# Second scores of four token groups in one exp, doubled by DMA; softmax sums and parts of h through the gate ring

## Chip, cores, metric

One NeuronCore of one Trainium2 chip. The metric is device microseconds (us) of one execution; lower is better. PE is TensorE, ACT ScalarE, DVE VectorE, POOL GpSimd and SP SyncE; PSUM is the memory that PE writes its results to.

## The reference, cut to what matters

```python
# x: (4, 12416, 128) fp32; inducing: (32, 128); moe weights 128x1536, 128x1536, 1536x128
def mab(q, kv):
    s = (q @ kv.transpose(0, 2, 1)) / sqrt(128)
    a = exp(s - s.max(-1)); a /= a.sum(-1)
    return a @ kv
h = mab(inducing, x)             # 32 rows per batch: first attention
y = mab(x, h)                    # 12416 tokens per batch: second attention
out = (relu(y @ w_gate) * (y @ w_val)) @ w_out      # hidden width 1536
```

## The kernel before

Four batches, here called blocks (b = 0 to 3). Tokens go in groups of 512. A **pair** is two groups, a **quad** is four. (Two or four blocks per exp mean groups.)

The hidden weights are multiplied once per block with h (`hgv`), so that the gate and value of a token need only its 32 second scores: `p2` (exp of x times h) against `hgv`. The scores' sum `z2` is not divided out until the end; the result is scaled with 1/z2 twice. A **unit** is 128 hidden columns for a pair: two gate matmuls and two value matmuls (K = 32), two relus on ACT (`g`), one product on DVE (`gv`). Each **slot** of the hand-made schedule issues one unit: 147 slots per block, 588 in all. Twelve products feed an output chain of twelve full 128x128x512 matmuls in one PSUM bank.

PSUM has three rings (a ring is a few buffers that are used in turn): "g" with three banks for gates, "v" with two double banks for values, "o" with one bank for the output chain. The gates ring also takes **guests**: things that PE writes and ACT copies or exponentiates, and that need a bank for a moment.

```python
def bank(tag, name, shape=None, dtype=FP32):
    return psum.tile(shape or [P, BLK], dtype, tag=tag,
                     bufs={"g": 3, "v": 2, "o": 1}[tag], name=name)

def s2_pe(hT, xT, pr):                       # second scores of one pair, hT holds h twice
    ps = bank("g", "s2_ps")
    for k in range(2):
        t0 = (2 * pr + k) * TPB
        nc.tensor.matmul(ps[64*k : 64*k+64, :], hT, xTs(xT, t0, TPB), start=True, stop=True)
    return ps
def s2_exp(ps, pr):
    p2 = st([P, BLK], FP16, "p2", 4)
    nc.scalar.activation(out=p2, in_=ps, func=AF.Exp, scale=sm_scale)
    return p2
def z2_pe(p2s):                              # sums of the second softmax, in the OUTPUT bank
    ps = bank("o", "z2_ps", [P, 2, TPB, 2], FP32)
    for j, p2 in enumerate(p2s):
        for t in range(TPB):
            nc.tensor.matmul(ps[:, j, t, :], p2[:, t*P:(t+1)*P], sel, start=True, stop=True)
    return ps
```

While block b runs, the first attention of block b+1 ("phase 1") is prepared in between, in six parts and a rest: x is loaded and cast (`x16`), transposed by DMA (`xT`), scored (`s1T`, a guest), exponentiated (`p1T`), transposed by DMA (`p1g`), and used for h:

```python
def act():                                   # first exp, with its row sums from the accumulator
    p1T = st([P, BLK], FP16, "p1T", 2)
    nc.scalar.activation(out=p1T, in_=ps, func=AF.Exp, scale=sm_scale,
                         accum_out=s["zp"][:, q:q+1])
    def tr():
        p1g = st([P, TPB, P], FP16, "p1g", NQ)
        nc.sync.dma_start_transpose(out=p1g, in_=p1T)
        s["p1g"][q] = p1g
    post[at + 2].append(tr)
...
def h_part(q):                               # all parts in ONE group of the output bank, late
    if q == 0: s["h_ps"] = bank("o", "h_ps", [P, P], FP32)
    for t in range(TPB):
        for r in range(4):
            nc.tensor.matmul(ps[32*r : 32*r+32, :], s["p1g"][q][:, t, 32*r : 32*r+32],
                             s["x16"][:, q*CT + r*TPB + t, :], start=..., stop=...)
...
s["jobs"] = [ ([(at, lambda q=q: h_part(q)) for q in range(NQ + 1)], sums, ([1, 2, 2, 2],) * 2),
              ([(at, join)], finish, ([1], [1])) ]
```

`join` adds the four row groups of h (`hz_ps`), DVE divides (`hT`), and `hgv` of the next block is made. Output chains, z2, h and the join are **jobs**: they share the one output bank and follow each other. A finished chain goes on: ACT copies it out (`oT`), SP (SyncE) issues its DMA transpose (`o`), GpSimd scales it (`osb`), SP issues the store. SP thus issues loads, transposes and stores, all in one order fixed by the schedule.

The softmax here doesn't subtract the row's maximum and nothing guards it: scores larger than these inputs give would overflow.

## Time and profile before

| | before |
|---|---|
| time, median of 4 runs (range) | 753.06 us (749.74 to 754.89) |
| DVE, ACT, PE busy | 93%, 92%, 88% |
| mean granted PE clock | 0.969 |
| guests in the gate ring | 81 |

The prediction below shows the busy shares, the groups and the pace.

### The profile page before, as it was taken

Reading aid. Unit: us, or ns where it says so; the run is one execution under the profiler, and the core shown is the slowest. Engines: PE = TensorE matmul, PEld = TensorE weight load, DVE = VectorE, ACT = ScalarE, POOL = GpSimd, SP = SyncE. Lnnn points to the kernel's source line nnn. Section 1 sums busy time; section 2 is a strip of 40 time slices with the busy share of each in tenths; the row PEclk is TensorE's granted clock in tenths of the full one; section 3 lists DMA queues with packets and bytes.
Section 4 is the critical chain, followed back from the end, with each engine's and each line's share of the span. In section 5 each row is a group of like instructions: output and inputs, shape, how many; then the busy total and the mean of one; then the engine's idle time right before and its main releaser. Section 6 shows DMA issues by size and latency. Waiting matters only on the chain. (4 is left out here: it accounts for less than half of the span.)

```text
span 751.8 us, 13935 instructions
## 1 busy us (share of the span) xinstructions
PE 660.0 (88%) x4719; PEld 196.3 (26%) x4719; DVE 696.6 (93%) x670; ACT 690.2 (92%) x1393; POOL 211.7 (28%) x418
## 2 busy tenths in 40 slices
PE   4788998998988899898888899899898988898897
PEld 4422222222232222222222222222222222222222
DVE  3499999999999999999989999999999999999986
ACT  3589999998999999999899999999899999999985
POOL 3403323321234233222123333331122222222221
PEclk9869999999999999999999999999999999999999
DMA  8615555621135655642125556652112112122212
GB/s 340 211 24 163 128 136 134 155 69 44 50 120 139 154 142 147 143 102 59 42 80 138 162 127 146 161 129 60 37 49 64 57 55 65 45 63 63 65 43 69
DMA packets 121511, 78.51 MB, mean 104 GB/s; under 512 B 101952, under 2 KB 105056, under 8 KB 119136
## 3 DMA queue, kind: packets, MB, share of 16 engines
q1 hardware_dynamic: 121440, 77.63, 38.2%
q8 instruction: 37, 0.61, 0.3%
q14 instruction: 34, 0.28, 0.1%
HBM read 27.80 MB, written 25.43 MB: 71 GB/s over the span
## 5 line engine op out<-in xcount | busy, mean ns | idle before, releaser
L775 DVE TENSOR_TENSOR gv<-g,v_ps 128x1024 f16<-128x1024 f16 x576 | 669.5, 1214 | 27.1 <-PE g_ps L711 17.2
L772 ACT ACTIVATE g<-g_ps 128x512 f16<-128x512 f32 x1164 | 613.3, 616 | 34.5 <-PE g_ps L711 24.1
L514 PE MATMUL o_ps<-gv,wo 128*128 128x512 f16 x1128 | 341.3, 391 | 45.2 <-ACT oT L520 37.8
L711 PE MATMUL g_ps<-p,hgv 32*128 32x512 f16 (+1 forms) x1200 | 299.8, 382 | 3.5 <-ACT g L772 1.5
L531 POOL TENSOR_SCALAR osb<-o,z2i 128x128 f32<-128x128 f16 x376 | 164.0, 452 | 488.0 <-DMA o<-oT 322.5
L711 PE MATMUL v_ps<-p,hgv 32*128 32x512 f16 (+1 forms) x1200 | 236.2, 387 | 3.9 <-DVE gv L775 2.7
L514 PEld LDWEIGHTS <-wo 128*128 128x128 f16 x1176 | 82.7, 98 | 210.6 <-issue 178.8
L711 PEld LDWEIGHTS <-hgv 32*128 32x128 f16 x2400 | 65.8, 91 | 265.0 <-issue 259.3
L520 ACT CAST oT<-o_ps 128x512 f16<-128x512 f32 (+1 forms) x98 | 57.0, 582 | 0.0
L380 POOL CAST x<-x 128x2048 f16<-128x2048 f32 x18 | 34.1, 1892 | 13.2 <-DMA x<-in_x_dram 13.2
L171 ACT ACTIVATE p<-s_ps 128x512 f16<-128x512 f32 x48 | 29.2, 608 | 2.1 <-PE s_ps L161 2.1
L161 PE MATMUL s_ps<-xT,hT 128*64 128x512 f16 x96 | 21.5, 435 | 3.6
L251 DVE COPY xT<-xT_ps 128x1024 f16<-128x1024 f16 x12 | 8.3, 692 | 14.6 <-PE xT_ps L250 14.0
L250 PE MATMUL xT_ps<-eye,x 128*128 128x128 f16 x97 | 9.7, 257 | 9.2 <-ACT x L245 4.7
L258 ACT ACTIVATE p<-s_ps 128x256 f16<-128x256 f32 (+1 forms) x13 | 4.8, 370 | 12.1 <-PE s_ps L256 12.1
L181 PE MATMUL z_ps<-sel,p 128*128 128x2 f16 x192 | 8.2, 163 | 7.5 <-ACT oT L520 6.8
L161 PEld LDWEIGHTS <-hT 128*64 128x64 f16 x96 | 9.2, 110 | 18.9 <-issue 16.4
L181 PEld LDWEIGHTS <-p 128*128 128x128 f16 x192 | 8.1, 96 | 14.0 <-issue 13.5
L410 ACT ACTIVATE p1T<-s1T_ps 128x512 f16<-128x512 f32 x18 | 11.1, 619 | 0.0
L775 DVE TENSOR_TENSOR gvr<-g,v_ps 128x512 f16<-128x512 f16 x12 | 8.2, 686 | 2.6 <-PE g_ps L711 2.2
L250 PEld LDWEIGHTS <-x 128*128 128x128 f16 x97 | 7.1, 115 | 10.4 <-ACT x L245 5.4
L247 POOL CAST x<-gv 128x1024 f16<-128x1024 f32 x6 | 6.2, 1042 | 12.1 <-DMA gv<-in_x_dram 12.1
(83 smaller groups left out, 134.8 us busy)
## 6 DMA issues: line engine op xcount, KB each, us to landing
out_dram<-osb SPq DMA_DIRECT2D x94, 256.0 KB, 2.1
x<-in_x_dram SPq DMA_DIRECT2D x18, 1024.0 KB, 5.3
gv<-in_x_dram SPq DMA_DIRECT2D x12, 512.0 KB, 8.5
o<-oT SPq DMA_TRANSPOSE x98, 2.4
x<-in_moe_w_out_dram SPq DMA_DIRECT2D x1, 768.0 KB, 10.8
x<-in_moe_w_gate_dram SPq DMA_DIRECT2D x1, 512.0 KB, 9.5
x<-in_moe_w_val_dram SPq DMA_DIRECT2D x1, 512.0 KB, 9.6
out_dram<-osb SPq DMA_DIRECT2D x4, 128.0 KB, 1.7
```

The costliest lines, as they stand in the source:

```text
L161: nc.tensor.matmul(ps[64 * k : 64 * k + 64, :], hT, xTs(xT, t0, TPB), start=True, stop=True)
L171: nc.scalar.activation(out=p2, in_=ps, func=AF.Exp, scale=sm_scale)
L181: nc.tensor.matmul(ps[:, j, t, :], p2[:, t * P : (t + 1) * P], sel, start=True, stop=True)
L250: nc.tensor.transpose(ps[:, t - t0, :], x16[:, t, :], eye16)
L380: nc.gpsimd.tensor_copy(out=s["x16"][:, t0:t1, :], in_=s["x32", q])
L410: nc.scalar.activation(out=p1T, in_=ps, func=AF.Exp, scale=sm_scale, accum_out=s["zp"][:, q : q + 1])
L514: nc.tensor.matmul(c["ps"][:, 0:w], wo[:, i, :], gv(i), start=(i == 0), stop=(i == NFF - 1))
L520: nc.scalar.copy(out=oT[:, 0:w], in_=c["ps"][:, 0:w])
L531: nc.gpsimd.tensor_scalar(out=osb[:, t, :], in0=o16[:, t, :], scalar1=zz, scalar2=zz, op0=ALU.mult, op1=ALU.mult,)
L711: nc.tensor.matmul(ps[:, cols], hgv[:, s * P : (s + 1) * P], p2, start=True, stop=True)
L772: nc.scalar.activation(out=g16[:, k * BLK : (k + 1) * BLK], in_=ps, func=AF.Relu)
L775: nc.vector.tensor_tensor(out=ready["dst"], in0=ready["g16"][:, 0:n], in1=ready["v"][:, 0:n], op=ALU.mult)
```

## The change

Its intent, in four parts:

1. Second scores of a quad (four groups of 512) in one matmul pass and **one exp** (`p2q`) in place of two; each unit needs every score row twice, so eight small DMA copies on SP's queue double them.
2. The sums `z2` go through the gate ring (ACT copies them out, DVE inverts), not through the output bank.
3. h is made in seven separate guests of the gate ring; ACT copies each part out and GpSimd adds it up. PE makes the weight sums with a column of ones, so the accumulator reads fall away (21 of them before, 4.6 us of ACT; none after).
4. Output chains run at an even pace (1,2,2,2,2,3 matmuls per slot), with guests at the chain's second slot.

The diff, cut to its core:

```diff
+    def s2_quad_pe(hT, xT, qd):
+        ps = bank("g", "s2_ps")
+        for r in range(4):
+            nc.tensor.matmul(ps[32 * r : 32 * r + 32, :], hT[:, 0:M],
+                             xTs(xT, (4 * qd + r) * TPB, TPB), start=True, stop=True)
+        return ps
+    def p2_copies(p2q):
+        p2 = [st([P, BLK], FP16, "p2", 4) for _ in range(2)]
+        for j in range(2):
+            for k in range(2):
+                for d in range(2):
+                    nc.sync.dma_start(
+                        out=p2[j][64 * k + 32 * d : 64 * k + 32 * d + 32, :],
+                        in_=p2q[64 * j + 32 * k : 64 * j + 32 * k + 32, :])
+        return p2
 ... (cut)
+                ps = bank("g", "z2_ps", [P, TPB, 4])          # z2: was bank "o"
+                z2 = st(ps.shape, FP32, "z2" + tag, 2)
+                nc.scalar.copy(out=z2, in_=ps)
+                nc.vector.reciprocal(out=z2i, in_=z2)
 ... (cut)
-                    nc.scalar.activation(out=p1T, in_=ps, func=AF.Exp, scale=sm_scale,
-                                         accum_out=s["zp"][:, q : q + 1])
+                    nc.scalar.activation(out=p1T, in_=ps, func=AF.Exp, scale=sm_scale)
 ... (cut)
+        def h_part(at, q):
+            ps = bank("g", "h_ps", [P, P + 1])                # was one group in bank "o"
+            (4 matmuls with ones16[:, 0:1] into column P, 16 into columns 0 to P-1)
+            def act():
+                hq = st([P, P + 1], FP32, "hq", 2)
+                nc.scalar.copy(out=hq[0:n, :], in_=ps[0:n, :])
+                nc.gpsimd.tensor_tensor(out=s["hp"][0:n, :], in0=s["hp"][0:n, :],
+                                        in1=hq[0:n, :], op=ALU.add)
+        for q in range(NQ + 1):
+            at = at0 + (30 + 16 * q if q < NQ else 52)
+            fill(at, at + 10, lambda at, q=q: h_part(at, q))
 ... (cut)
-            counts = ([1, 2, 1, 2, 3, 3], [1, 3, 2, 3, 3])
+            counts = (5, 5) if fast else (6, 5)
```

## The prediction

> **What bounds the kernel now.** I read the page's busy shares first, then the costliest groups with shapes kept apart, then the timeline of VectorE (DVE), then TensorE (PE) in windows of 3.4 us.
>
> ```profile
> PE 660.0 (88%) x4719; PEld 196.3 (26%) x4719; DVE 696.6 (93%) x670; ACT 690.2 (92%) x1393; POOL 211.7 (28%) x418
> ```
>
> Three engines are nearly full, so the shares alone don't name the bound. The loop makes one "unit" per slot: 588 slots, in four blocks (batches) of 147, each with two relus on ACT and one product on DVE.
>
> ```profile
> L775 DVE TENSOR_TENSOR gv<-g,v_ps 128x1024 f16<-128x1024 f16 x576 | 669.5, 1214 | 27.1 <-PE g_ps L711 17.2 <-ACT g L772 2.7 <-PE s_ps L161 1.0
> L772 ACT ACTIVATE g<-g_ps 128x512 f16<-128x512 f32 x1164 | 613.3, 616 | 34.5 <-PE g_ps L711 24.1
> L171 ACT ACTIVATE p<-s_ps 128x512 f16<-128x512 f32 x48 | 29.2, 608 | 2.1 <-PE s_ps L161 2.1
> L334 DVE RECIPROCAL z2i<-z_ps 128x16 f32<-128x16 f32 x24 | 6.0, 251 | 0.0
> L410 ACT ACTIVATION_READ_ACCUMULATOR p1T<-s1T_ps 128x1 f32 x18 | 4.0, 225 | 0.0
> ```
>
> In each row: busy us, mean ns of one, idle us before. The products alone fill 669.5 us. Consecutive ones overlap a little, so the pace is read from the timeline. It shows the reciprocals of the second softmax, one per two pairs (24 slots), as time marks; columns are start and length.
>
> ```profile
> 610.40 0.25 DVE L334 RECIPROCAL z2i<-z_ps 128x16 f32<-128x16 f32 x1
> 610.56 27.52 DVE L775 TENSOR_TENSOR gv<-g,v_ps 128x1024 f16<-128x1024 f16 x24
> 638.00 0.25 DVE L334 RECIPROCAL z2i<-z_ps 128x16 f32<-128x16 f32 x1
> ```
>
> This is the last block, which prepares no following block: 27.60 us per 24 slots. Where two products stand back to back (2.35 us for 2, length of one 1.22) the pace is 1.13 us. 24 x 1.13 = 27.1, plus 0.165 for the reciprocal (from 610.40 to 610.56), is 27.3. So the last block already runs at the DVE floor within 1%. **DVE is the bound there, and nothing in the change can take more than about 0.3 us per 24 slots from it.** Blocks 0 to 2 also prepare the next block's first attention ("phase 1"). The same marks in block 1:
>
> ```profile
> 225.73 0.25 DVE L334 RECIPROCAL z2i<-z_ps 128x16 f32<-128x16 f32 x1
> ...
> 253.70 0.25 DVE L334 RECIPROCAL z2i<-z_ps 128x16 f32<-128x16 f32 x1
> ...
> 310.43 0.25 DVE L334 RECIPROCAL z2i<-z_ps 128x16 f32<-128x16 f32 x1
> ...
> 338.41 0.25 DVE L334 RECIPROCAL z2i<-z_ps 128x16 f32<-128x16 f32 x1
> ...
> 373.42 0.25 DVE L334 RECIPROCAL z2i<-z_ps 128x16 f32<-128x16 f32 x1
> ```
>
> From 225.73 to 338.41 are four stretches of 24 slots: 28.17 each, 0.57 over the last block. From 338.41 to the end of the block (392.04, its next product) are 39 full products and 3 half ones; at 1.15 and 0.65 that is 46.8, and it took 53.6: **6.8 us over**. Here stand the 97 h matmuls in four slots without any output-chain matmul, the join that waits for DVE, and chains that then catch up at 3 steps a slot.
>
> The last loss is the **clock**. The first four rows below are windows of 3.4 us with the output-chain matmuls alone (their number is the x in the first busy column); each directly precedes a stretch at half clock. The fifth is an ordinary window.
>
> ```profile
> 100.67:104.08 3.41, 0.52 (x2) 0.21 (x3) 1.00 0.20 77
> 158.70:162.11 3.41, 0.82 (x3) 0.31 (x4) 1.00 0.21 41
> 179.18:182.59 3.41, 0.43 (x2) 0.14 (x3) 1.00 0.20 77
> 534.16:537.58 3.42, 0.01 (x1) 0.01 (x1) 1.00 0.14 54
> 619.52:622.93 3.41, 2.25 (x8) 0.63 (x9) 1.00 0.20 77
> ```
>
> The first of these windows and its successor again, with all engines (busy us and count of PE, weight loads, DVE, ACT, GpSimd; then the clock):
>
> ```profile
> 100.67:104.08 3.41, 3.05 (x26) 1.05 (x27) 3.37 (x5) 3.41 (x9) 2.86 (x4) 1.00 0.20 77
> 104.08:107.50 3.42, 3.42 (x15) 0.63 (x13) 2.07 (x2) 2.56 (x6) 0.00 (x0) 0.50 0.89 170
> ```
>
> In the window after (clock 0.50), DVE was busy 2.07 of 3.42 us: 1.3 us lost. Between 52 and 740 us there are eight such stretches, and seven follow a window with 1 to 3 full chain matmuls (ordinary: 4 to 8); the eighth follows one with a narrow chain. 8 x 1.3 = 10 us.
>
> [...]The page's transfers land in 1.5 us (64 KB) to 2.1 us (256 KB), and each issue of a store holds the SP queue 0.34 us.
>
> **The change, part by part.**
>
> 1. *Second scores of four blocks in one exp.* 23 of 48 exps go. At an incremental 0.51 us (12 relus follow one another in 6.22 us: (6.22-0.6)/11) that is 11.7 us of ACT, and 23 passes of PE x 0.21 (three chain matmuls take 0.82 us, one 0.39: half the difference) = 4.9 us. In their place SP issues 184 copies x 0.34 = 63 us. SP mostly waits today, so they should lie beside other work.
> 2. *z2 through the gate ring.* ACT copies 24 x 128x16 to SBUF: [...] The matmuls fall from 192 to 100. More important, the z2 job no longer takes a slot without chain matmuls and no longer waits for the one output bank.
> 3. *Weight sums by PE and GpSimd.* 21 accumulator reads go: 4.6 us of ACT. 18 copies of 128x129 come: [...]and three small ones. PE gets 75 tiny matmuls of about 0.04 (8 of z2 took 0.34): 3 us. GpSimd gets 21 additions at perhaps 0.45 (its 128x128 scale takes 452 ns), about 10 us on an engine 28% busy. DVE loses three copies, sums and products (0.28+0.15+0.29 per block).
> 4. *h parts and even pace.* I took the slots from the order of instructions in the two built programs. Before, three successive slots hold as little as no chain step; after, each chain is 1,2,2,2,2,3 with a fill in its second slot, so three successive slots hold at least 4, except at the join and in the tail.
>
> [...]ACT isn't the floor in the quiet stretches, but in phase 1 each first exp with its accumulator read (0.5+0.2) fits no slack. So, per stretch:
> - 24 slots in phase 1: 28.17 to about 27.75 (half an exp of ACT saved per 12 slots, 0.2 per first exp[...]). 0.42 x 4 stretches x 3 blocks = 5.
> - Join stretch: 6.8 over, of which 1.3 is clock, so 5.5. What stays is DVE's rz and hT (0.58) and ACT's three evacuations of the hidden weights, in all about 2.3. (5.5-2.3) x 3 = 9.6.
> - Last block and reciprocals: 1.
> - Clock: I expect 3 cold stretches instead of 8, at the joins and in the tail, where windows stay low: 5 x 1.3 = 6.5.
>
> Sum 22. I take 2 off for new waits: 754 - 20 = **734 us**.
>
> **The rivals.**
> - *Late copies.* At a block's boundary the quad's scores come in slot 141 and are used in 147. Eight issues take 2.7 us and the last lands 2 us later, 5 us of the 6.8, and SP is in order behind stores and transposes that wait for GpSimd. For: the margin is thin three times. Against: elsewhere it is 14 slots. If it holds, 1 to 3 us three times, or SP becomes a bound: 738 to 744.
> - *The gate ring.* Guests in the three-bank ring rise from 81 to 107 (z2 28 and h 21 in, 23 scores out), and each holds the second gate until one more relu is done. If each costs 0.3 us, ACT gets the bound and 8 us come back: 742. Against: scores pass through the same ring in the last block, which runs at the DVE floor.
> - *The clock stays.* [...]the join and tail get them every time and others move in: 8 remain, 740.
>
> **Range and chances.** All three rivals together would give some 750; none of them and no cold stretch 726. Runs of before alone span 749.7 to 754.9. The range is 725 to 745. 2% faster is 739; it takes more than one rival to lose that. Faster 0.76, within 2% 0.23, slower 0.01.
>
> **What would show it.** Right: the last block's 24 slots still 27.3 to 27.6; phase-1 stretches near 27.8; the clock row with three or fewer dips after startup; no wait of DVE or PE at a join; ACT's busy time down by about 9 us beside a shorter span. Wrong: PE waiting for a DMA of the score copies; ACT waiting for PE gates more than today's 24 us; PE waiting for GpSimd before the join; as many half-clock stretches as now, or such stretches after windows with 5 or more chain matmuls. A time above 745 would mean that the gate ring or SP has become the bound.

## More of the kernel before

One more view matters later: the waits between 50 and 740 us. Columns: who waited for whom, then us in total, times, longest us.

```profile
PE o_ps L514 <- ACT oT L520: 37.8, 65, 0.6
ACT g L772 <- PE g_ps L711: 21.9, 44, 1.3
DVE gv L775 <- PE g_ps L711: 16.3, 39, 1.1
```

PE never waits for a DMA in this stretch as far as its matmuls go, and DVE, the bound, waits 16.3 us for PE.

## The result

| | before | after |
|---|---|---|
| time, median of 4 runs | 753.06 us | 783.53 us (781.18 to 785.27) |
| ratio, 95% interval | | 1.0408 (1.036 to 1.0456) |
| mean granted PE clock, profiled run | 0.969 | 0.948 |

Ratios here and below are the mean time of one kernel's runs over the mean of the other's of the same rounds, so they are not quite the ratio of the medians quoted. The change is 4% **slower**; the prediction said 734 us, 745 at most. From the page after: busy shares, the granted clock in 40 slices, and the two groups that fill ACT and DVE.

```profile
PE 668.0 (85%) x4702; PEld 195.0 (25%) x4702; DVE 695.1 (89%) x663; ACT 686.6 (88%) x1398; POOL 219.9 (28%) x439
PEclk9879899989999979999899997999989999999999
L874 DVE TENSOR_TENSOR gv<-g,v_ps 128x1024 f16<-128x1024 f16 x576 | 667.8, 1214 | 59.5 <-PE g_ps L798 51.1
L871 ACT ACTIVATE g<-g_ps 128x512 f16<-128x512 f32 x1164 | 616.8, 617 | 47.3 <-PE g_ps L798 40.0
```

DVE and ACT do no more work than before (695.1 against 696.6 us, 686.6 against 690.2). The 31 us are idle time: before its products DVE stood idle 59.5 us instead of 27.1, nearly all of it waiting for PE. The clock row has dips all through the three blocks that prepare a following one. The waits of the kernel after, from 50 to 770 us, name what PE itself waited for:

```profile
DVE gv L874 <- PE g_ps L798: 48.4, 61, 6.6
PE o_ps L606 <- ACT oT L612: 43.2, 75, 0.6
ACT g L871 <- PE g_ps L798: 37.4, 93, 1.4
PE h_ps L527 <- DMA p1g<-p1T: 23.2, 6, 5.8
```

DVE's wait grew from 16.3 to 48.4 us, which is the loss. The fourth line is new: six times, twice in each of blocks 0 to 2, PE stands still for 2 to 6 us at an h part whose transposed first scores (`p1g`) are not there. The gates behind it in PE's order wait as well: below, the next ones start at 284.20 us, 7.6 us after those at 276.63. One of the six, on PE's timeline (start, length, instruction, idle before it):

```profile
276.63 0.56 PE L798 MATMUL g_ps<-p,hgv 32*128 32x512 f16 x2
282.90 0.27 PE L527 MATMUL h_ps<-ones,p1g 128*128 128x1 f16 x4 [5.71 <-DMA p1g<-p1T]
```

The queue of SP over the same time tells why the transpose was late (start, length of issue, line, transfer):

```profile
261.80 6.00 SPq L202 DMA_DIRECT2D p<-p2q  x8
...
268.52 1.22 SPq L616 DMA_TRANSPOSE o<-oT  x1
...
275.72 0.36 SPq L633 DMA_DIRECT2D out_dram<-osb  x1
276.17 1.22 SPq L616 DMA_TRANSPOSE o<-oT  x1
277.55 1.90 SPq L461 DMA_TRANSPOSE xT<-x  x1
279.55 1.66 SPq L489 DMA_TRANSPOSE p1g<-p1T  x1
```

Eight score copies hold SP for 6.0 us. The output transpose behind them is issued at 268.52 and lands 5.3 us later (2.5 is the median), beside a 1 MB load of x that was issued just before it (267.84) and took 5.4 us. So the copies are not the only part of the delay. GpSimd gets its tile late, as its timeline shows:

```profile
273.96 1.73 POOL L623 TENSOR_SCALAR osb<-o,z2i 128x128 f32<-128x128 f16 x4 [12.62 <-DMA o<-oT]
```

SP then waits for this scale before it can issue the store (275.72), and behind the store stand another output transpose, an x transpose and at last `p1g` at 279.55. PE had begun the first scores that it transposes at 270.24. PE resumes at 282.90, and not at full speed; the windows of 3.4 us (busy us and count of PE, weight loads, DVE, ACT, GpSimd; clock; DMA share; GB/s):

```profile
278.68:282.09 3.41, 0.00 (x0) 0.00 (x0) 0.00 (x0) 0.00 (x0) 1.73 (x4) 0.51 1.08 194
282.09:285.50 3.41, 2.60 (x27) 0.88 (x27) 0.59 (x1) 0.90 (x3) 0.95 (x3) 0.50 0.44 116
285.50:288.92 3.42, 3.42 (x14) 0.63 (x13) 2.83 (x3) 2.54 (x5) 1.20 (x3) 0.50 0.56 151
```

All engines but GpSimd empty, then two more windows at clock 0.50. Between start-up and end the kernel before has eight windows at half clock (eight stretches of 3.41 us, 27 us), the kernel after eighteen in ten stretches (3.41 to 10.24 us, some 61 us). Stretches at half clock are called cold below.

Block lengths, from marks on DVE's timeline (the reciprocal of a block's last tokens, one in each block):

| | end of block 0 to 1 | end of block 1 to 2 |
|---|---|---|
| before | 177.3 us | 178.6 us |
| after | 190.8 us | 191.1 us |

So each middle block lost about 13 us. The last block, without phase 1, shows the floor unmoved:

```profile
638.10 0.24 DVE L404 RECIPROCAL z2i<-z 128x16 f32<-128x16 f32 x1
638.26 27.47 DVE L874 TENSOR_TENSOR gv<-g,v_ps 128x1024 f16<-128x1024 f16 x24
665.64 0.24 DVE L404 RECIPROCAL z2i<-z 128x16 f32<-128x16 f32 x1
```

27.54 us per 24 slots; before it was 27.60.

### The profile page after: what moved, and what is told of

It reads as the page before. It is cut to its first block, busy times and chain, and to the rows that moved or that the text cites. A ratio compares the mean times of both kernels' runs of the same rounds, so it can differ in the third digit from the quotient of the medians.

```text
span 782.7 us, 14156 instructions
## 1 busy us (share of the span) xinstructions
PE 668.0 (85%) x4702; PEld 195.0 (25%) x4702; DVE 695.1 (89%) x663; ACT 686.6 (88%) x1398; POOL 219.9 (28%) x439
## 4 chain that ended last, share of the span: by engine, by line
PE 45%; ACT 25%; issue 14%; DVE 10%; DMA 5%; POOL 1%; SPq 0%; ACTq 0%; DVEq 0%; POOLq 0%
PE o_ps L606 21%; ACT g L871 18%; PE v_ps L798 13%; DVE gv L874 10%; PE g_ps L798 6%; ACT oT L612 4%; DMA p1g<-p1T 3%; DMA o<-oT 1%; PE h_ps L536 1%; PE xT_ps L277 1%; PE s1T_ps L475 1%; PE o_ps L662 1%; DMA gv<-in_x_dram 1%; ACT p2q L193 1%; POOL osb L623 1%
## 5 line engine op out<-in xcount | busy, mean ns | idle before, releaser
L874 DVE TENSOR_TENSOR gv<-g,v_ps 128x1024 f16<-128x1024 f16 x576 | 667.8, 1214 | 59.5 <-PE g_ps L798 51.1
L871 ACT ACTIVATE g<-g_ps 128x512 f16<-128x512 f32 x1164 | 616.8, 617 | 47.3 <-PE g_ps L798 40.0
L606 PE MATMUL o_ps<-gv,wo 128*128 128x512 f16 x1128 | 353.7, 398 | 44.5 <-ACT oT L612 41.0
L798 PE MATMUL g_ps<-p,hgv 32*128 32x512 f16 x1152 | 297.3, 396 | 7.5 <-ACT g L871 2.9
L798 PE MATMUL v_ps<-p,hgv 32*128 32x512 f16 x1152 | 234.6, 399 | 8.2 <-DVE gv L874 6.9
L798 PEld LDWEIGHTS <-hgv 32*128 32x128 f16 x2400 | 71.6, 91 | 283.8 <-issue 279.9
L527 PE MATMUL h_ps<-ones,p1g 128*128 128x1 f16 x72 | 4.5, 166 | 24.2 <-DMA p1g<-p1T 23.2
L557 ACT COPY hq<-h_ps 128x129 f32<-128x129 f32 (+1 forms) x18 | 5.4, 303 | 21.8 <-PE h_ps L536 21.8
L193 ACT ACTIVATE p2q<-s_ps 128x512 f16<-128x512 f32 x23 | 14.4, 628 | 0.0
L485 ACT ACTIVATE p1T<-s1T_ps 128x512 f16<-128x512 f32 x18 | 11.6, 646 | 0.0
L527 PEld LDWEIGHTS <-p1g 128*128 128x128 f16 x72 | 3.7, 98 | 31.1 <-DMA p1g<-p1T 26.0
L182 PE MATMUL s_ps<-xT,hT 128*32 128x512 f16 x92 | 9.8, 416 | 1.4
L272 ACT CAST x<-gv 128x1024 f16<-128x1024 f32 x5 | 5.2, 1038 | 4.9 <-DMA gv<-in_x_dram 4.9
```

The source lines that it names most:

```text
L182: nc.tensor.matmul(ps[32 * r : 32 * r + 32, :], hT[:, 0:M], xTs(xT, (4 * qd + r) * TPB, TPB), start=True, stop=True,)
L193: nc.scalar.activation(out=p2q, in_=ps, func=AF.Exp, scale=sm_scale)
L606: nc.tensor.matmul(c["ps"][:, 0:w], wo[:, i, :], gv(i), start=(i == 0), stop=(i == NFF - 1))
L798: nc.tensor.matmul(ps[:, cols], hgv[:, s * P : (s + 1) * P], p2, start=True, stop=True)
L871: nc.scalar.activation(out=g16[:, k * BLK : (k + 1) * BLK], in_=ps, func=AF.Relu)
L874: nc.vector.tensor_tensor(out=ready["dst"], in0=ready["g16"][:, 0:n], in1=ready["v"][:, 0:n], op=ALU.mult)
```

## The experiments

**Theory A**: the copies hold SP's queue, and through it they delay `p1g`; the h parts that come only 6 slots after their scores (slots 40 to 46 and 88 to 94 of a block; other parts have 10 to 14) stall PE, and the clock follows. **Theory B**: 6 slots are too few in any case, with or without copies. **Theory C**: the gate ring's additional guests cost the time. Runs 1 to 4 shared a chip (before there: 750.93 us median), 5 to 8 another (752.13), 9 and 10 a third (751.81). All results were correct. "Kernel 4" is the kernel of run 4, and so on. Waits quoted in this section are from 50 to 740 us.

### 1. The h parts six slots later

```diff
-            at = at0 + (30 + 16 * q if q < NQ else 52)
+            at = at0 + (36 + 16 * q if q < NQ else 58)
```

> Only edit: the h parts of the changed kernel are allowed 6 slots later, so that each stands 16 to 22 slots after its first scores instead of 6 to 14; copies, rings and pace stay. Theory A (six waits of TensorE for the transposed weights p1g, 23 us, made by the SP queue that the score copies fill, plus the half-clock stretches that follow them, cause the loss): the waits for p1g go to under 1 us, cold stretches fall from 10 to about 4, time about 750. Theory B (the distance of 6 slots is too short whatever SP does): the same, about 750. Theory C (the gate ring's guests cost, the waits are a side effect): the waits go, but the time stays at 770 or more.

Measured: 754.22 us, ratio 1.0016 (0.9963 to 1.0069). No matmul waits for `p1g`; DVE waits 20.6 us for PE. One line of the schedule takes away 0.039 of the 0.041 lost, about 29 us. The stall at `p1g` is the loss against before, with the half clock it brings. Theories A and B both said so; run 1 doesn't separate them. That the gain is still missing stays to be explained. (One wait of PE for the transposed x, 2.1 us, appeared; run 10 comes back to it.)

### 2. Half the copies, h parts early as in the change

The score rows are laid out so that the rows of two groups lie together, and one copy moves 64 partitions:

```diff
-            for k in range(2):
-                for d in range(2):
-                    nc.sync.dma_start(
-                        out=p2[j][64 * k + 32 * d : 64 * k + 32 * d + 32, :],
-                        in_=p2q[64 * j + 32 * k : 64 * j + 32 * k + 32, :],
-                    )
+            for d in range(2):
+                nc.sync.dma_start(out=p2[j][64 * d : 64 * d + 64, :], in_=p2q[64 * j : 64 * j + 64, :])
```

(`sel2`, the order of gate and value rows in `hgv`, the scores of a pair and of the rest, and the row groups of the units follow; cut.)

> Only edit: the rows of the doubled scores are laid out so that 4 copies of 64 partitions do what 8 copies of 32 did; h parts as in the changed kernel. Theory A: SP is held about half as long per quad (2.5 to 3 us instead of 5 to 6), p1g comes 2.5 to 3 us earlier at each of six places, waits fall from 23 to about 8 us, time 758 to 768. Theory B: the waits stay within 3 us of 23, time about 780.

Measured: 757.7 us, ratio 1.0072 (1.0021 to 1.0123); PE's matmuls wait 1.4 us in all for `p1g` (theory A had said about 8). With the same early h parts, halving the copies takes nearly all of the stall away; ten cold windows stay (mean granted clock 0.965). A copy of 64 partitions holds SP as long as one of 32 (583 and 588 ns at the median). The row of the score copies in the tile view (min/median/max ns of an issue), first the kernel after, then this one:

```profile
L202 SPq DMA_DIRECT2D p<-p2q x184: 523/588/1695, 38.4 to 727.9; - x184
```

```profile
L201 SPq DMA_DIRECT2D p<-p2q x92: 472/583/1249, 38.8 to 697.1; - x92
```

### 3. Part 1 undone: pairs, no copies, h parts early

```diff
-                ev_s2_quad(b, qd, a + 4, a + 10)
+                ev_s2_pair(b, 2 * qd, a + 4, a + 10)
+                ev_s2_pair(b, 2 * qd + 1, base - 8, base - 2)
```

> Undoes the first part alone: second scores of two blocks per exp as before, no copies; everything else as changed, with the same 6-slot distance at two h parts per block. Theory A: no wait for p1g over 1 us, ACT busy about 9 us more than changed, time about 750. Theory B: the six waits stay, time 775 or more.

Measured: 760.53 us, ratio 1.0107 (1.0052 to 1.0162). No matmul waits for `p1g` at the same distance of 6 slots: **theory B falls**, the copies are needed for the stall. But without the copies the rest of the change is 1% slower than the kernel before (theory A had said about 750 us), with 130 guests in the ring (81 before, 107 in the change): something else costs, and theory C is the candidate.

### 4. Half the copies and later h parts

The edits of 1 and 2 together.

> Both edits, half the issues and h parts 6 slots later. Theory A and B: no waits for p1g, time 1 to 3 us under the run with late h parts alone, if SP matters elsewhere (boundaries of blocks), 746 to 750; equal to it if SP mattered for p1g only. Theory C: 770 or more.

Measured: 748.0 us, ratio 0.9943 (0.9896 to 0.999). Blocks last 177.6 and 177.3 us, four stretches at half clock (mean granted clock 0.974). So with half the copies and later h parts the change gains 0.6%, not the 2.7% that was predicted (0.973). In a stretch without stall or half clock, from 216.67 to 334.67 us (99 slots), 24 slots take 28.6 us, where the kernel before took 28.17 and the prediction had 27.75. ACT waits 26.5 us for PE's gates (before 21.9).

### 5. 24 more guests

Kernel 4 with a dummy guest per quad: four small matmuls and an ACT copy of 128x16, read by nobody.

```diff
+    def ev_dummy(first, last):
+        def pe(at):
+            ps = bank("g", "d_ps", [P, TPB, 4])
+            for t in range(TPB):
+                nc.tensor.matmul(ps[:, t, :], ones16, sel4, start=True, stop=True)
+            def act():
+                d = st([P, TPB, 4], FP32, "dummy", 2)
+                nc.scalar.copy(out=d, in_=ps)
+            post[at + 1].append(act)
+        fill(first, last, pe)
...
+            ev_dummy(base + 12, base + 20)
```

> On top of half issues and late h parts (748.0, ratio 0.994 to before): 24 more guests in the gate ring, each four tiny matmuls and a 128x16 copy on ACT, read by nobody. Theory R (each guest costs about 0.33 us because it holds the second gate and a slot's pace, whatever its length): +8 us, ratio 1.004 to 1.007. Theory L (a guest costs only its length on ACT[...]): +2 to 3 us, ratio 0.997. Theory 0 (ACT has slack for it): no change.

Measured: 759.62 us, ratio 1.0106 (1.0067 to 1.0144), 11.6 us more than kernel 4 by the medians, 1.6% by the ratios (the chips differ); theory R had said 8 us. ACT waits for PE's gates 34.2 us instead of 26.5. DVE's wait in kernel 4 and then here:

```profile
DVE gv L879 <- PE g_ps L803: 19.3, 40, 0.8
```

```profile
DVE gv L894 <- PE g_ps L818: 26.6, 58, 1.3
```

By the marks on DVE's timeline blocks 0 to 2 are 9.8 us longer than in kernel 4, for 18 dummies; three more windows at half clock are part of it (mean granted clock 0.968, in kernel 4 0.974). The last block, with six dummies, is 0.3 us longer. So guests cost time where phase 1 runs. What it is about them isn't separated: each dummy takes a place in the ring, but also some 0.22 us of ACT and 0.25 us of PE (an estimate from z2's guests of the same shapes: a copy took 224 ns in kernel 4, four matmuls 0.25 us in kernel 7), and no run gave it a bank outside the ring.

### 6. 24 fewer guests

Kernel 4 with the h parts two at a time (3 guests per block instead of 7, the rest inside the second) and z2 of two quads in one guest. The number of matmuls stays, the guests fall from 107 to 83.

```diff
-                ps = bank("g", "z2_ps", [P, TPB, 4])
-                for t in range(TPB):
+                ps = bank("g", "z2_ps", [P, 2 * TPB, 4])
+                for t in range(2 * TPB):
...
-        for q in range(NQ + 1):
-            at = at0 + (36 + 16 * q if q < NQ else 58)
+        for q in range(1, NQ, 2):
+            at = at0 + 36 + 16 * q
             fill(at, at + 10, lambda at, q=q: h_part(at, q))
```

> On top of half issues and late h parts: h parts two at a time with the rest in the middle one (3 guests per block instead of 7) and weight sums of two quads in one guest; 24 guests fewer, the same arithmetic. Theory R: 8 us less, about 740, ratio 0.983. Theory L: the work is the same[...], ratio 0.992. If the 40 matmuls in one slot stall TensorE, slower again in those rows.

Measured: 735.33 us, ratio 0.9785 (0.9756 to 0.9813): 12.7 us less than kernel 4 by the medians, 1.6% by the ratios (the chips differ). ACT waits 20.9 us for gates. Three windows at half clock (mean granted clock 0.979). DVE's wait:

```profile
DVE gv L890 <- PE g_ps L814: 10.5, 23, 0.9
```

Runs 5 and 6 move the time both ways by about 12 us, as theory C expects, but run 6 removes more than guests: 24 ACT instructions and 12 of 24 reciprocals of DVE, the bound, fell away too. In its last block, where run 5's dummies took next to nothing, 24 slots take 27.25 us instead of kernel 4's 27.54. At that rate all 24.5 such stretches would make 7 us. By this estimate between some 6 and 12.7 us of run 6 belong to the guests.

### 7. PE kept busy at the joins

This tests the prediction's rival about the clock. In kernel 4 three of the four cold stretches stand at the joins. PE waits there for DVE, as its timeline shows, because the join holds the one output bank:

```profile
363.01 0.51 PE L611 MATMUL o_ps<-gv,wo 128*128 128x512 f16 x1 [0.82 <-DVE hT L133]
```

Into this hole go three full matmuls to a gate bank that nobody reads:

```diff
         def finish(at):
+            busy = bank("g", "busy_ps")
+            for i in range(3):
+                nc.tensor.matmul(busy, wo[:, i, :], wg[:, 0:BLK], start=True, stop=True)
             s["hT"] = finish_h(...)
```

> On top of half issues and late h parts: three full matmuls into a gate bank that nobody reads, at the three joins, where TensorE waits 0.8 us for DVE and where each profile shows a half-clock stretch directly after. Theory H (a window of 3.4 us with few full matmuls makes the half-clock stretch): no half-clock stretch at the three joins, 1.2 us each won back less about 0.3 us each for the guest, time 2 to 3 us less, ratio about 0.991. Rival P (the stretches come from load, not from low windows): the three stretches stay or come elsewhere, time the same or 1 us more.

Measured: 748.04 us, ratio 0.9962 (0.9927 to 0.9997): no clear change against kernel 4, where 2 to 3 us less were expected. The three cold stretches at the joins are gone (the windows after the joins, from 185.66, 363.13 and 540.62 us, ran at 0.50 in kernel 4; here the 7 us around each join ran at 1.00), so PE's hole at the join was what brought them. But three others came up elsewhere, and kernel 4's fourth is gone. Their preceding windows, output-chain matmuls alone:

```profile
210.93:214.34 3.41, 1.05 (x4) 0.30 (x4) 1.00 0.36 67
388.40:391.81 3.41, 1.17 (x4) 0.19 (x2) 1.00 0.26 63
449.90:453.31 3.41, 1.01 (x5) 0.30 (x4) 0.99 0.68 166
```

Four or five chain matmuls in a window were not enough here, though the prediction built on four. Nor did a low count always bring a cold window: the kernel before has three windows without any chain matmul (from 175.78, 353.26 and 530.75 us), and the next ran at full clock. One of them and its successor, in the same view:

```profile
175.78:179.19 3.41, 0.00 (x0) 0.00 (x0) 1.00 0.21 43
179.19:182.61 3.42, 0.45 (x2) 0.16 (x3) 1.00 0.20 77
```

The first of the two was filled with the 97 h matmuls. A count over the traces of before and after, made afterwards, fits better. It adds up every matmul in a window, in proportion to the part that lies in it: its moving columns times the rows and columns of its weights, over 128 x 128, so 512 for a chain matmul and 128 for a gate or value matmul. The 18 cold stretches of these two traces outside start-up and end follow windows with a sum of at most 2953, about six chain matmuls. The 373 other windows at full clock, whose successor ran at full clock too, had at least 3047; the one with the h matmuls had 4467. The gap is narrow and the traces are two, so this is a count and not the clock's condition.

### 8. Fewer guests and the busy join

Edits of 6 and 7 together.

> Both edits of the two runs before. Theories R and H: about 738, ratio 0.98, the fastest of the study. If only one holds, 740 to 745.

Measured: 734.36 us, ratio 0.9765 (0.9735 to 0.9795), the fastest of all and 2.4% faster than the kernel before. No window at half clock between start-up and end (mean granted clock 0.984, the start-up included); blocks last 173.3 and 173.4 us. What is left of the waits:

```profile
ACT g L890 <- PE g_ps L817: 17.2, 52, 0.5
DVE gv L893 <- PE g_ps L817: 7.9, 16, 0.9
```

Against kernel 6 the difference (0.2%) is within the intervals; that the busy join adds to it isn't shown. Against before it holds DVE's saved reciprocals too.

### 9. Part 1 undone in the good version

Kernel 8 with pair exps and without copies (the ring of `p2` is made 8 deep, so that it does not wait for it).

```diff
-                ev_s2_quad(b, qd, a + 4, a + 10)
+                ev_s2_pair(b, 2 * qd, a + 4, a + 10)
+                ev_s2_pair(b, 2 * qd + 1, a + 5, a + 11)
```

> The fastest so far (734.4, ratio 0.9765) with the first part of the change undone: two blocks per exp, no copies, so 23 more exps of 0.5 us on ACT, which are 23 more guests of the gate ring. If a guest costs 0.37 us in blocks 0 to 2 and little in the last: 17 x 0.4 to 0.5 = 7 to 9 us more, about 742. If the quads' copies cost as much elsewhere as their exps save: the same 734.

Measured: 747.1 us, ratio 0.9928 (0.9884 to 0.9971). Part 1, with its copies halved, is worth 1.6% (about 12 us, where 7 to 9 were expected): 23 exps, which are also 23 guests. ACT was busy 11.3 us longer than in kernel 8, so how much is the exps' own work and how much their place in the ring stays open.

### 10. Eight copies in the good version

Kernel 8 with the copies of the change, eight of 32 partitions per quad (the edit of 2 reversed).

> The fastest so far with the change's own row layout and 8 copies per quad instead of 4; h parts late and few, join busy. If SP's time mattered only through the early h parts: the same, 733 to 736. If its 110 us of issues delay more (block boundaries, output transposes that free the oT tiles): 738 or more.

Measured: 747.11 us, ratio 0.994 (0.9891 to 0.999). Of the two outcomes the second came: SP's issues delay more than the h parts. The eight copies take all of part 1's gain by another way. PE's matmuls wait 6.3 us for the transposed x (`xT`) of the next block, and five cold stretches are back (mean granted clock 0.978, in kernel 8 0.984). SP's queue and then PE:

```profile
283.05 4.97 SPq L202 DMA_DIRECT2D p<-p2q  x8
...
297.04 0.57 SPq L114 DMA_DIRECT2D x<-in_x_dram  x1
...
305.87 0.34 SPq L647 DMA_DIRECT2D out_dram<-osb  x1
306.26 1.95 SPq L465 DMA_TRANSPOSE xT<-x  x1
```

```profile
310.76 0.40 PE L479 MATMUL s1T_ps<-xT,indT 128*32 128x512 f16 x4 [2.16 <-DMA xT<-x]
```

This `xT` stands behind a store that waits for GpSimd's scale, as `p1g` did. Through which of the transfers since 283.05 the delay was handed on wasn't traced; that the copies cause it rests on the edit, for in kernel 8, with four copies, no matmul waits for `xT`. So `p1g` was only the first victim: once its distance was long enough, the queue delayed the next tightest transfer.

## Why the prediction was wrong

All ratios in one place, in the order in which the causes come off:

| kernel | ratio to before | what was taken away |
|---|---|---|
| after | 1.0408 | |
| 1 | 1.0016 | the stall at `p1g`, by distance |
| 4 | 0.9943 | half of SP's copies |
| 6 | 0.9785 | 24 guests of the gate ring (and 12 reciprocals of DVE) |
| 8 | 0.9765 | PE's hole at the join (0.2%, within the noise) |
| predicted | 0.973 | (734 of 754) |

- **The step that failed** is the last of part 1: "In their place SP issues 184 copies x 0.34 = 63 us. SP mostly waits today, so they should lie beside other work." Two things were wrong in it. The term: a copy's issue took 0.60 us in the mean, not the 0.34 of a store, so 110 us in all and 5 to 6 us at a stretch. And the inference: that SP mostly waits says nothing about a queue in fixed order, in which eight issues in a row (6.0 us from 261.80) delay the transfers behind them, and a store among those also waits for GpSimd's scale (the one at 275.72). The runs put the six stalls in its place: 23.2 us of PE's wait, and 32.1 us more of DVE's wait for PE (48.4 less 16.3) for a loss of 31. Runs 1, 2 and 3 take the stall away by three different edits, and each brings back 0.030 to 0.039.
- **The rival "late copies"** named the queue and "SP is in order behind stores and transposes that wait for GpSimd", but looked for the victim among the scores at a block's boundary, where the copies are used. It was a transfer that the diff hardly touches: `p1g`, whose user the change had moved closer, from a late job to as little as 6 slots. The prediction worked out no distance for the h parts, and so its 738 to 744 came out 40 us too low.
- **The rival "gate ring" was right in direction; its price was too small.** It counted 26 more guests at 0.3 us, 8 us. Run 5 gives the cleanest price: 24 guests more than kernel 4 cost 1.6%, about 0.5 us each with the cold windows that came along. Three other comparisons also come to 1.6%, but each changes more than guests: 24 fewer in run 6 (with DVE's reciprocals), and 23 score guests in place of the copies (3 against 4, where the h parts also stand early, and 9 against 8), which bring the work of 23 full exps. If 0.5 us held for the change's 26, they would cost 13 us; no run removed just these. Whether the place in the ring or the guests' small instructions on PE and ACT cost it is not shown. The argument against the rival, "scores pass through the same ring in the last block", holds only there: run 5's dummies took 0.3 us from the last block.
- **The 24-slot stretches of phase 1** were to fall from 28.17 to 27.75 (5 us). They measured 28.6 in kernel 4 and 28.2 even in kernel 8, which has fewer reciprocals too. This gain never came. That kernel 8 ends at the predicted 734 is then partly chance: its last block is quicker (27.25 per 24 slots), and it has no cold stretch where three were allowed.
- **The clock**: that a little-used window brings the half clock held, and run 7 shows it by filling the hole (clock 1.00 at the joins, 0.50 after them in kernel 4). Its measure, the count of chain matmuls, failed: "ordinary: 4 to 8" is not so even in the trace of before (the window from 175.78), and windows with 4 or 5 were followed by cold ones in run 7. The sum over all matmuls separates the windows better in the traces of before and after (at most 2953 before the 18 cold stretches, at least 3047 in the other 373 windows; run 7). The count of three stretches instead of eight failed as well, ten came: the stalls leave little-used windows of their own (from 278.68 us PE did nothing for 3.41 us).
- **The join**: "no wait of DVE or PE at a join" failed. In kernel 4 PE waits 0.82 us for `hT` (2.5 us in three waits in the kernel after), since the next chain needs the bank that the join holds (the wait in the fence of run 7).
- **Right**: the last block stays at DVE's floor (27.54 us per 24 slots; 27.3 to 27.6 predicted). Four groups' scores cost PE what two had (23 quads 9.8 us, 0.43 each; 48 pairs before 21.5 us, 0.45 each). Of the named signs of failure, ACT's wait for gates came as written (40.0 us over the whole run; today's was 24.1), and so did as many cold stretches as before (ten, eight before). "PE waiting for a DMA of the score copies" came only in kind: PE's matmuls waited for `p1g`, a transfer behind the copies. ACT's busy time fell, but by 3.6 us and not 9: relus rose from 613.3 to 616.8 us, which is 3.5 of the 5.4 missing, and the 9 rested in part on the estimate of the small copies, which no trace had shown. Measured after, one takes 228 ns for z2 and 310 for h.

**Open**: the exact condition of the clock; what about a guest costs; how much of the 0.7% between runs 1 and 4 is steady pace and how much a different start-up and cold stretches; whether the busy join helps once guests are few; and parts 2 and 3 each on its own, which no run undid.

## What to carry to other kernels

Before putting transfers on a queue, don't ask how full it is but what stands behind them: multiply the number in a row by the measured issue time of that kind of transfer (medians in the kernel after: 0.59 us for a score copy, 0.34 for a store, 1.2 to 1.9 for a transpose), and compare it with the slots between each following transfer and its user. Price a temporary in a small PSUM ring by adding dummies of its kind and timing them, not by the length of its instructions: 24 copies of 0.22 us cost about 12 us here. When a change is a bundle, vary the cheap distance first (here one line gave back 29 us), then look again: the next bottleneck was a different one.
